# Attention with a gated residual on one core: five loads held until the third query group, and the last stores issued by ACT

## Chip, cores, metric

One Trainium2 chip, one core. The metric is the device time of one launch in microseconds. Lower is better. A profile belongs to one execution.

## The reference, cut to what matters

```python
xn  = layernorm(A_x)                       # 2048 x 448
q   = xn @ wq                              # 16 query heads of 256, 8 key/value heads
s   = softmax(q k^T / 16) v @ wo           # over the last 512 positions of the cache
g   = silu((gelu(xn @ w_gate) * (xn @ w_up)) @ w_down)
out = x + s * g
```

The gate g is worked out first and parked in DRAM. The attention then goes through four chunks of 512 rows with 16 heads each, and each chunk ends with `out = x + s*g`.

## The kernel before: the parts concerned

The kernel records operations in program order, and a helper works out the semaphore waits from the buffers. An operation therefore starts when its buffers are free, unless `after` gives it another operation to wait for.

```python
def op(self, eng, fn, reads=(), writes=(), dma=False, after=()):
    ...
    o.deps.extend(after)
```

One query group is a row of up to four pairs of q projections. Keys and values are loaded at the starts of groups. The first gates (g) and x tiles, which are read only at the ends of the first chunk (`burst_end` in the code, about 247 us), are recorded in the third group, on GpSimd's queue:

```python
if m == Q0 + QS and p == 0:                      # third group, after its first pair (m = 12)
    K.reuse(b_kT[6:] + b_va[5:] + [b for y in b_xr for b in y])
    for g in range(6, Hkv):
        load_k(g)                                # SyncE, transposing
    for g in range(5, Hkv):
        load_v(g)                                # SyncE
    for t in range(NG2):
        load_g2(t)                               # GpSimd, 2 x 112 KB
    for t in range(NXR):
        dma("pool", xr[:, t, :], x_view[:, t, :], (), b_xr[t])   # GpSimd, 3 x 112 KB
```

Recorded there, they are issued as soon as GpSimd's queue finds the buffers free. In the attention, each head's probabilities go through a transposing transfer from SBUF to SBUF on SyncE's queue (pT<-pn), two halves for each head, and the product with the values stands two heads later:

```python
dma_t(pT[:, x, t4 // 2, ...], pn[:, y, ...], (b_pn[y],), (b_pT[x][t4 // 2],))
...
if len(late) == LAG:        # LAG = 2
    pv(late.pop(0))         # reads va[g] and pT
```

The last halves of two output tiles are finished in three pieces, 224 columns of one tile and twice 112 columns of the other, each followed by its store:

```python
def last_end(t, c0, c1, i, b_i, f):
    ...
    add("dve", xs[:, t4, c0:c1], xs[:, t4, c0:c1], x[:, c0:c1], by + bx, by)
    dma("sp", out_view[:, t, c0:c1], xs[:, t4, c0:c1], by, ())
```

The pieces' (c0, c1) are (0, 224), (0, 112) and (112, 224), in this order.

The softmax here doesn't subtract the row's maximum and nothing guards it: scores larger than these inputs give would overflow.

Of the kernel before, what the change touches and what calls it, by code (L numbers as in the profile page):

```python
# [168 lines left out]
def bass_recurrent_scan__sliding_block_cached__geglu_ffn__prompt_kernel(  # L169
# [37 lines left out]
    N2 = D // 2  # L207
# [4 lines left out]
    with es:  # L212
        K = Plan(nc, es)
        base = [(nc.sbuf_base + 31) // 32 * 32]

        def place(name, shape, dt, at=None):
            size = {BF16: 2, F16: 2, F32: 4}[dt]
            for n in shape[1:]:
                size *= n
            size = (size + 31) // 32 * 32  # L220
            if at is None:
                at = base[0]
                base[0] += size
            assert at + size <= nc.sbuf_usable_end, (name, at + size, nc.sbuf_usable_end)
            return nc.alloc_sbuf_tensor_at(name, list(shape), dt, offset=at), at, at + size

        def sbuf_bufs(at, size, n):
            return [K.buf(at + i * size, size) for i in range(n)]
# [27 lines left out]
        NG2 = 2  # L256
        g2, a, _ = place("g2", [P, NG2, D], BF16)
        b_g2 = sbuf_bufs(a, D * 2, NG2)
        g2d = nc.dram_tensor("g2_all", [NT, P, D], BF16)
        b_g2d = [K.buf() for t in range(NT)]  # L260
# [8 lines left out]
        xr, a, _ = place("xr", [P, NXR, D], BF16)  # L269
        b_xr = [[K.buf(a + (i * D + lo) * 2, (hi - lo) * 2) for lo, hi in ((0, CUT), (CUT, D))] for i in range(NXR)]  # L270
# [95 lines left out]
        x_view = A_x.rearrange("b (t p) d -> p (b t) d", p=P)  # L366
        out_view = out.rearrange("b (t p) d -> p (b t) d", p=P)
# [5 lines left out]
            return n - g + (QS - Q0 if g == 0 else 0)  # L373


        def dma(q, o, i, reads=(), writes=()):
            K.op(q, lambda e, o=o, i=i: e.dma_start(o, i), reads, writes, dma=True)  # L377

        def dma_t(o, i, reads=(), writes=()):
            K.op("sp", lambda e, o=o, i=i: e.dma_start_transpose(o, i), reads, writes, dma=True)  # L380
# [4 lines left out]
        def add(eng, o, x, y, reads, writes, op=ALU.add):  # L385
            K.op(eng, lambda e: e.tensor_tensor(o, x, y, op), reads, writes)  # L386
# [10 lines left out]
        def load_x(q, t0, n):  # L397
            dma(q, x4[:, t0:t0 + n, :], x_view[:, t0:t0 + n, :], (), b_x4[t0:t0 + n])
# [185 lines left out]
        def sum_act(c, k, i=None):  # L584

            fs = {0: slice(0, 4), 1: slice(4, NH), None: slice(0, NH)}[i]
            o = lambda e, r: (actTh[:, c % 2, e * NH + fs.start:e * NH + fs.stop, r * HC:(r + 1) * HC],
                              b_actT[c % 2][e * NH + fs.start:e * NH + fs.stop])
            S = lambda j: (dn[c][0][j][0][:, fs, :], dn[c][0][j][1] if len(dn[c][0][j][1]) == 1 else dn[c][0][j][1][fs])
            j, (x, bx), (y, by), op = ((3, o(0, 0), o(0, 1), ALU.subtract), (2, o(1, 1), S(3), ALU.subtract),  # L590
                                       (0, S(2), o(0, 0), ALU.add), (1, o(1, 0), S(2), ALU.subtract))[k]
            add("dve", S(j)[0], x, y, bx + by, S(j)[1], op)
# [127 lines left out]
        def load_k(g):  # L720
            dma_t(kT[:, g, :, :], A_k_cache[0, g, Sk - W:Sk, :], (), (b_kT[g],))

        def load_v(g):
            dma("sp", va[:, g, :, :],
                A_v_cache[0, g, Sk - W:Sk, :].rearrange("(j p) d -> p j d", p=P), (), (b_va[g],))
# [90 lines left out]
        def q_group(n, pairs, more_act=False):  # L816

            c, h = divmod(n, Hq)
            units = [(b, lambda j, k, i=i: wq[:, k, (h + i) * Dh + j * P:(h + i) * Dh + (j + 1) * P],
                      wqr[:, h + i, :], slice(c * QC, (c + 1) * QC), b_wql[h // HG][:1], b_wql[h // HG][1:], b_xnT[c * 4:c * 4 + 4])  # L820
                     for i, b in enumerate(pairs)]
            group(units, 0, QC, True, True)
            for i, b in enumerate(pairs):
                s = qs(n + i)
                act(qT[:, s, 0, :], bank[b], ACT.Copy, (b_ps[b],), (b_qT[s][0],))
                if more_act and i:
                    act(qT[:, s, 1, :], bank[b + 1], ACT.Copy, (b_ps[b + 1],), (b_qT[s][1],))
                    continue
                K.op("dve", lambda v, s=s, b=b: v.tensor_copy(qT[:, s, 1, :], bank[b + 1]),  # L829
                     (b_ps[b + 1],), (b_qT[s][1],))  # L830
# [41 lines left out]
        xs = xnT[:, :, 0:D]  # L872
        o_view = oTh.rearrange("p (h e) (r q) -> p e r h q", e=2, r=2)

        def load_g2(t):
            dma("pool", g2[:, t % NG2, :], g2d[t], (b_g2d[t],), (b_g2[t % NG2],))

        def burst_end(t, ns=(0, 1)):

# [13 lines left out]
        def last_end(t, c0, c1, i, b_i, f):  # L893

            t4, x, g = t % 4, xr[:, t % NXR, :], g2[:, t % NG2, :]
            bx, by = b_xr[t % NXR][:1], [K.buf()]
            by[0].old.extend(b_xs[t4][0].readers + [b_xs[t4][0].writer])
            K.op("dve", lambda e: e.scalar_tensor_tensor(  # L898
                out=xs[:, t4, c0:c1], in0=i, scalar=f, in1=g[:, c0:c1], op0=ALU.mult, op1=ALU.mult), (b_i, b_g2[t % NG2]), by)
            add("dve", xs[:, t4, c0:c1], xs[:, t4, c0:c1], x[:, c0:c1], by + bx, by)  # L900
            dma("sp", out_view[:, t, c0:c1], xs[:, t4, c0:c1], by, ())

        def burst(c):

# [106 lines left out]
        for m in range(NS):  # L1011
            if m in groups:
                hi = groups[groups.index(m) + 1]
                three = hi - m == 6
                for i in range(m, hi, 2):
                    end = m > Hq and m % Hq == LAG
                    p = (i - m) // 2
                    q_group(i, ((cur, nxt[::-1], (cur[1], nxt[1])) if three else (cur, nxt) * 2)[p], end)
                    if m == 0:
                        sum_act(2, 2 + p)  # L1020
                    if m == Q0 and p == 0:
                        K.reuse(b_kT[2:6] + b_va[3:5])
                        for g in range(2, 6):
                            load_k(g)
                        for g in range(3, 5):
                            load_v(g)
                    if m == Q0 and p < 2:
                        gates3(2 * p)
                        gates3(2 * p + 1)
                    if m == Q0 + QS and p == 0:  # L1030
                        K.reuse(b_kT[6:] + b_va[5:] + [b for y in b_xr for b in y])
                        for g in range(6, Hkv):
                            load_k(g)
                        for g in range(5, Hkv):
                            load_v(g)
                        for t in range(NG2):
                            load_g2(t)
                        for t in range(NXR):
                            dma("pool", xr[:, t, :], x_view[:, t, :], (), b_xr[t])
                    if end and p:  # L1040
                        burst_end((m // Hq - 1) * 4 + p - 1)
                    if m > Hq and m % Hq == LAG + QS and p == 1:
                        burst_end((m // Hq - 1) * 4 + 3)
                if m == 0:
                    K.reuse([b for x in b_pT for b in x] + b_pn + b_p32)
            if m > Hq and m % Hq == LAG:
                K.reuse(b_pn + b_p32)
            s_mm(m)
            if m < LAG:
                if m == 0:  # L1050
                    gates2 = down7(2, (BB[0], BB[1], AB[2], AB[3], BB[2], BB[3]), g2w, b_g2w, (3, 4, 6, 5, 2, 1),
                                   lambda: [sum_act(3, k) for k in range(4)])
                else:
                    gates3 = down7(3, (BB[1], BB[0], AB[2], AB[3], BB[2], BB[3]), g2w, b_g2w, (3, 4, 2, 5, 6, 1),
                                   lambda: [gates2(q) for q in range(4)])
                    K.reuse(b_pT[2])
                if m == LAG - 1:
                    K.reuse(b_oT + [b for y in b_qT[:QS - Q0] for b in y])
                    assert not CASTS and not SUMS
            if len(late) == LAG:  # L1060
                pv(late.pop(0))
            if m > Hq and m % Hq == LAG - 1:
                if m // Hq == 1:
                    for b in [y for x in b_xs for y in x]:
                        b.old.extend(y for t in range(4) for z in b_xnT[t] for y in z.readers + [z.writer])
                burst(m // Hq - 1)
            late.append(m)
# [56 lines left out]
```

## Time and profile before

| | before |
|---|---|
| time, median of 4 runs with the changed kernel's | 543.56 us (543.03 to 544.43) |
| profiled span | 541.5 us |
| TensorE idle in the middle | one wait, 1.03 us, ending at 170.07 |
| last VectorE add to the span's end (called the tail from here on) | 538.93 to 541.55: 2.6 us |

The prediction shows the lines and how they are read.

### The profile page before, as it was taken

How to read it: one execution, taken by the hardware profiler on the slowest of the kernel's cores; microseconds unless marked ns; L12 is line 12 of the kernel's file. 1: busy time of each engine (PE TensorE's matmuls, PEld its weight loads, DVE VectorE, ACT ScalarE, POOL GpSimd, SP SyncE). 2: the span in 40 equal slices, each digit the busy share in tenths (PEclk: the TensorE clock that was granted, in tenths of full speed). 3: DMA queues.
4: the chain of work that ended last, by engine and by line, in shares of the span. 5: the costliest groups of instructions: out<-in, count | busy, mean ns of one | idle time of the engine just before them, and what ended most of it. 6: DMA issues, size and time to landing. Idle time of an engine off the chain costs nothing.

```text
span 541.5 us, 10848 instructions
## 1 busy us (share of the span) xinstructions
PE 535.7 (99%) x4138; PEld 306.3 (57%) x4138; DVE 376.3 (69%) x825; ACT 313.4 (58%) x780; POOL 39.5 (7%) x78
## 2 busy tenths in 40 slices
PE   8999999999999999999999999999999999999997
PEld 5554457449644444884444469544444984444587
DVE  6673885799767757934875786467667934776775
ACT  5433854873667858206875860388488216876820
POOL 1130400000002000003001000120100003001010
PEclk9999999999999999999999999999999999999999
DMA  9569261921487767302781670066457402873731
GB/s 298 120 186 130 45 142 41 301 64 42 113 189 159 157 145 149 77 1 69 164 156 45 148 146 1 18 142 153 96 105 150 67 1 72 167 151 82 135 71 35
DMA packets 171604, 61.38 MB, mean 113 GB/s; under 512 B 155104, under 2 KB 168416, under 8 KB 171552
## 3 DMA queue, kind: packets, MB, share of 16 engines
q1 hardware_dynamic: 167776, 51.39, 43.7%
q0 software_dynamic: 3008, 8.72, 6.9%
q8 instruction: 33, 0.54, 0.4%
q10 hardware_dynamic: 768, 0.57, 0.3%
q14 instruction: 19, 0.16, 0.1%
HBM read 19.76 MB, written 3.67 MB: 43 GB/s over the span
## 4 chain that ended last, share of the span: by engine, by line
PE 97%; DMA 1%; DVE 0%; issue 0%; ACT 0%; ACTq 0%
PE bank L392 97%; DMA pT<-pn 1%; DMA x<-in_A_x_dram 0%; DVE stats L439 0%; PE bank L490 0%; DVE xn L465 0%; DVE mv L442 0%; ACT p L844 0%; PE bank L509 0%; DVE xnT L898 0%; DVE xnT L386 0%; DVE rstd L459 0%; ACTq L155 0%
## 5 line engine op out<-in xcount | busy, mean ns | idle before, releaser
L844 ACT ACTIVATE p<-bank 128x512 f32<-128x512 f32 x256 | 150.6, 596 | 28.2 <-DVE pn L851 26.4
L392 PE MATMUL bank<-pT,va 128*128 128x512 bf16 x512 | 120.8, 379 | 1.0 <-DMA pT<-pn 1.0
L392 PE MATMUL bank<-kT,qT 128*128 128x512 bf16 x512 | 121.0, 379 | 0.0
L851 DVE TENSOR_SCALAR pn<-p,rden 128x512 bf16<-128x512 f32 x256 | 113.0, 484 | 8.2 <-DMA pT<-pn 3.9
L392 PE MATMUL bank<-xnT,wq 64*128 64x512 bf16 x768 | 94.9, 376 | 0.0
L392 PEld LDWEIGHTS bank<-pT,va 128*128 128x128 bf16 x512 | 49.9, 98 | 61.5 <-DMA pT<-pn 2.2
L392 PEld LDWEIGHTS bank<-kT,qT 128*128 128x128 bf16 x512 | 49.4, 98 | 61.7 <-issue 3.4
L392 PE MATMUL bank<-xnT,wgu 64*128 64x512 bf16 (+2 forms) x768 | 83.9, 350 | 0.1
L383 ACT ACTIVATE qT<-bank 128x512 bf16<-128x512 f32 x76 | 44.1, 596 | 51.9 <-PE bank L392 50.3
L829 DVE CAST qT<-bank 128x512 bf16<-128x512 f32 x52 | 34.9, 690 | 49.6 <-PE bank L392 49.6
L392 PEld LDWEIGHTS bank<-xnT,wq 64*128 64x128 bf16 x768 | 36.7, 94 | 46.3 <-ACT p L844 2.1
L392 PEld LDWEIGHTS bank<-xnT,wgu 64*128 64x128 bf16 x768 | 36.9, 94 | 36.8 <-issue 0.6
L848 DVE RECIPROCAL rden<-rsum 128x2 f32<-128x2 f32 x128 | 21.2, 165 | 47.4 <-ACT p L844 47.2
L844 ACT ACTIVATION_READ_ACCUMULATOR p<-bank 128x1 f32 x256 | 51.6, 202 | 0.0
L392 PE MATMUL bank<-wt,sr 128*128 128x224 f16 x512 | 50.0, 259 | 0.0
L383 ACT ACTIVATE gl<-bank 128x512 bf16<-128x512 f32 x56 | 33.1, 596 | 28.5 <-PE bank L392 26.1
L392 PEld LDWEIGHTS bank<-wt,sr 128*128 128x128 f16 x512 | 49.0, 98 | 0.4 <-ACT oTh L383 0.2
L869 DVE TENSOR_SCALAR oTh<-bank 128x512 f16<-128x512 f32 x62 | 42.4, 684 | 0.0
L383 ACT ACTIVATE oTh<-bank 128x512 f16<-128x512 f32 x66 | 38.9, 590 | 4.1 <-PE bank L392 4.1
L392 PE MATMUL bank<-wt,oTh 128*128 128x224 f16 (+1 forms) x416 | 38.4, 252 | 0.0
L392 PEld LDWEIGHTS bank<-wt,oTh 128*128 128x128 f16 x416 | 37.2, 98 | 0.9
L377 POOL DMA_DIRECT2D g<-g_all x14 | 7.8, 556 | 379.9 <-DVE xnT L386 285.0
(82 smaller groups left out, 403.7 us busy)
## 6 DMA issues: line engine op xcount, KB each, us to landing
wtb<-in_A_wo_dram POOLq DMA_DIRECT2D x4, 896.0 KB, 10.4
wq<-in_A_wq_dram SPq DMA_DIRECT2D x2, 1536.0 KB, 7.2
va<-in_A_v_cache_dram SPq DMA_DIRECT2D x8, 256.0 KB, 5.2
pT<-pn SPq DMA_TRANSPOSE x128, 2.7
xr<-in_A_x_dram POOLq DMA_DIRECT2D x15, 112.0 KB, 2.4
wd<-in_B_w_down_dram SPq DMA_DIRECT2D x1, 1568.0 KB, 7.9
g<-g_all POOLq DMA_DIRECT2D x14, 112.0 KB, 2.3
out_dram<-xr POOLq DMA_DIRECT2D x12, 112.0 KB, 2.2
```

What stands on the lines that cost most here:

```text
L377: K.op(q, lambda e, o=o, i=i: e.dma_start(o, i), reads, writes, dma=True)
L383: K.op("act", lambda e, o=o, i=i: e.activation(o, i, func, scale=scale), reads, writes)
L392: ins = e.matmul(o, lhsT=l, rhs=r, start=st, stop=sp, skip_group_check=True)
L829: K.op("dve", lambda v, s=s, b=b: v.tensor_copy(qT[:, s, 1, :], bank[b + 1]), (b_ps[b + 1],), (b_qT[s][1],))
L844: K.op("act", lambda e, b=b, r=r, z=z: e.activation(p32[:, z, :], bank[b], ACT.Exp, scale=att_scale, accum_out=rsum[:, r:r + 1]), (b_ps[b] ...
L848: K.op("dve", lambda e, r=r: e.reciprocal(rden[:, r - 1:r + 1], rsum[:, r - 1:r + 1]), b_rsum[r - 1:r + 1], b_rden[r - 1:r + 1])
L851: K.op("dve", lambda e, r=r - 1 + t, z=(n - 1 + t) % NP32, y=y, t=t: e.tensor_scalar(pn[:, y, t, :], p32[:, z, :], rden[:, r:r + 1], None, ...
L869: K.op("dve", lambda v, i=i, b=b: v.tensor_scalar(oTh[:, i, :], bank[b], WS, None, op0=ALU.mult), (b_ps[b],), (b_oT[i],))
```

## The change

The intent is to keep five GpSimd loads away from the transposes of the second group, and to let the last store leave without waiting for SyncE's queue. Cut to its core:

```diff
-            dma("sp", out_view[:, t, c0:c1], xs[:, t4, c0:c1], by, ())
+            dma("sp" if c1 < N2 else "act", out_view[:, t, c0:c1], xs[:, t4, c0:c1], by, ())
...
+                        now = [[o for o in K.ops if o.eng == "pe"][-1]]
                         for t in range(NG2):
-                            load_g2(t)
+                            load_g2(t, now)
                         for t in range(NXR):
-                            dma("pool", xr[:, t, :], x_view[:, t, :], (), b_xr[t])
+                            dma("pool", xr[:, t, :], x_view[:, t, :], (), b_xr[t], now)
```

`now` is the last TensorE operation recorded so far, that is the first pair of the third group. The rest of the diff passes `after` through. With N2 = 224, the first and the third store go to ACT, the second stays on SyncE.

More of the change, by code (lines that the diff above doesn't have):

```diff
@@ L373, in qs, with dma @@
             return n - g + (QS - Q0 if g == 0 else 0)
-        def dma(q, o, i, reads=(), writes=()):
-            K.op(q, lambda e, o=o, i=i: e.dma_start(o, i), reads, writes, dma=True)
+        def dma(q, o, i, reads=(), writes=(), after=()):
+            K.op(q, lambda e, o=o, i=i: e.dma_start(o, i), reads, writes, dma=True, after=after)
         def dma_t(o, i, reads=(), writes=()):
@@ L873, in bass_recurrent_scan__sliding_block_cached__geglu_ffn__prompt_kernel, with load_g2 @@
         o_view = oTh.rearrange("p (h e) (r q) -> p e r h q", e=2, r=2)
-        def load_g2(t):
-            dma("pool", g2[:, t % NG2, :], g2d[t], (b_g2d[t],), (b_g2[t % NG2],))
+        def load_g2(t, after=()):
+            dma("pool", g2[:, t % NG2, :], g2d[t], (b_g2d[t],), (b_g2[t % NG2],), after)
         def burst_end(t, ns=(0, 1)):
```

## The prediction

> **What bounds the kernel now.** I read the page first: the busy shares and the chain of work that ended last.
>
> ```profile
> PE 535.7 (99%) x4138; PEld 306.3 (57%) x4138; DVE 376.3 (69%) x825; ACT 313.4 (58%) x780; POOL 39.5 (7%) x78
> PEclk9999999999999999999999999999999999999999
> PE 97%; DMA 1%; DVE 0%; issue 0%; ACT 0%; ACTq 0%
> ```
>
> TensorE is busy for 535.7 of 541.5 us at full granted clock, and the chain is 97% matmul. Everything that can be won without fewer matmuls lies in the 5.8 us when TensorE is idle: the start, holes in the middle, and the end. Neither half of the change touches a matmul, so I looked for the holes. The list of TensorE's waits has one in the middle, and the chain in order of time says where it stands:
>
> ```profile
> PE bank L392 <- DMA pT<-pn: 1.0, 1, 1.0
> ```
>
> ```profile
> 164.73 5.29 DMA pT<-pn
> 170.02 0.05 issue
> 170.07 368.31 PE bank L392 x2592
> 538.37 0.02 issue
> 538.40 0.29 DVE xnT L898
> 538.68 0.02 issue
> 538.71 0.22 DVE xnT L386
> ```
>
> The columns are start, duration, what. One transposing transfer of the attention probabilities (pT<-pn) took 5.29 us; page part 6 gives 2.7 us as the median of all 128. After it, TensorE runs for 368 us without a hole, so the stall and the tail after 538.4 are the only two places where this change can act. The timeline around the stall shows what else was under way:
>
> ```profile
> 162.59 1.32 POOL L377 DMA_DIRECT2D g<-g_all  x2 [94.99 <-DVE rden L848]
> 163.90 1.59 POOL L377 DMA_DIRECT2D xr<-in_A_x_dram  x3
> ...
> 170.07 1.90 PE L392 MATMUL bank<-pT,va 128*128 128x512 bf16 x8 [1.03 <-DMA pT<-pn]
> ```
>
> GpSimd issues exactly the five loads that the change moves at 162.6 to 165.5, and the transposes issued at 163.28 and 164.73 fall among them; TensorE then waits 1.03 us. The DMA view of the slice 166.5 to 167.5 shows who had the DMA engines (queue, packets, MB, share of 16 engines):
>
> ```profile
> q0 software_dynamic: 31, 0.08, 46.1%
> q1 hardware_dynamic: 14, 0.00, 0.9%
> ```
>
> GpSimd's queue q0 is moving data while the transposes' q1 is all but at a standstill. So I take the five loads as the cause of the stall. Nothing reads them before the first burst end at about 247 us, so their delay costs nothing by itself.
>
> **What the Trainium skill says.** All three points are from "DMA: Bandwidth & Descriptors". Its section "Anatomy of one DMA — SWDGE (gpsimd) path" puts a GpSimd transfer at about 2.0 us plus bytes over 436 GB/s, so 2.3 us for 112 KB; the medians in the trace agree, 2.3 us for g and 2.4 us for xr. The three xr loads at 164 us took 4.1 to 4.3 us, so these were not alone. Its section "Queues, rings and completion order" says that each DMA engine goes round-robin between queues, a packet at a time. The slice above is less even than that, 46.1 to 0.9, so I can't count on fair sharing. Its section "Issuing engines are not separate DMA queues" says that another issuing engine saves only sequencer time to initiate. That is exactly what the second part of the change can win, so the question is how much SyncE time stands in front of the last store.
>
> **Part 1, what it removes.** The instruction order of the two programs differs on GpSimd only in what the first loads wait for: TensorE's semaphore instead of VectorE's; no instruction moves on TensorE or VectorE. Without the loads the transpose issued at 164.73 should land after 2.7 us, at 167.4. The matmul that needs it would follow the scores that run from 167.15 to 169.04. That is 1.6 us of room, so the whole stall goes: -1.03 us.
>
> **Part 1, what it adds.** The loads now wait for the last matmul of the first pair of q projections in the third query group. In the trace of before this pair ends near 192.3 (pairs take 3.02 us, the ACT copies of their results start at 191.76, 194.78 and 197.80). So the loads would be issued from 192.4 to about 195.1 on that scale. There they meet other transfers, as the timeline shows:
>
> ```profile
> 191.45 2.65 SPq L380 DMA_TRANSPOSE kT<-in_A_k_cache_dram  x2
> 194.14 1.68 SPq L377 DMA_DIRECT2D va<-in_A_v_cache_dram  x3
> 198.34 1.90 PE L392 MATMUL bank<-kT,qT 128*128 128x512 bf16 x8
> 200.08 1.89 PE L392 MATMUL bank<-pT,va 128*128 128x512 bf16 x8
> ```
>
> These are the keys of key/value heads 6 and 7 and the values of 5, 6 and 7. The matmul at 200.08 belongs to query head 10, two behind the scores of head 12; its key/value head is 5, so it reads the first of these three va loads. The tile view gives 4.2 us from its issue at 194.14 to its landing, so it lands at 198.3 and has only 1.7 us of room. The kT load needed at 198.34 lands at 195.3 (3.8 us after 191.45), 3 us of room. Other va loads are needed 7 us later. No pT is issued between 190.16 and 201.39, which must be why this place was chosen.
>
> How late will the va load be? The five loads' own DMA work: in the slice 162 to 168 q0 moved 0.51 MB in 45.2% of 6 us, 2.7 us of all 16 engines, so about 3.0 us for 0.57 MB. The DMA share from 193 to 198 in the view by stretches is 0.85 to 1.07 in every microsecond, so there are no free slots to take this up. By likeness: the pT transfer issued 2.1 us after the first load was late by 5.29 - 2.7 = 2.6 us; va is issued 1.7 us after the first load. The extremes are 3.0 us (all of q0's work goes first) and 1.5 us (even sharing). I choose 2.3 us, which is 0.6 us more than the room: +0.6 us of new TensorE stall, between 0 and 1.3.
>
> **Part 2, the tail.** The last three stores are ready at 537.64, 538.14 and 538.93, when the VectorE adds end. SyncE issues them in turn:
>
> ```profile
> 538.16 1.17 SPq L377 DMA_DIRECT2D out_dram<-xnT  x1
> ```
>
> The others took 0.33 and 0.43 us of the sequencer. The slow one is why the last store goes out at 539.38, not at 538.95; the tile view gives 1.6 us to its landing, 540.95, and the span ends at 541.5. One instruction fetch lies in this stretch (q8, one packet of 0.02 MB), and the store issued at 537.05 also took 2.9 us against 1.6 of its neighbour, so one held-up DMA engine is the likely reason, which blocked SyncE's queue. In the changed kernel the first and the third of these stores stand on ACT, whose last work is long past and whose two issues have no other DMA near. The third then leaves at 538.95 and lands at about 540.5. The middle one stays on SyncE and lands at 538.16 + 2.3 = 540.45 as before, so the gain can't exceed 0.5 us: -0.4 us.
>
> **Sum.** 543.99 - 1.03 + 0.6 - 0.4 = 543.16, so 543.1.
>
> **Rivals.** (a) No new stall. Work for va is queued while only g loads are in flight, and the DMA share can go above 1 (1.4 was seen at 166 to 167), so some overlap is possible; the kernel gains the full 1.4 us: 542.5 to 542.6. Against: the room is 1.7 us and the only measured likeness says 2.6. (b) The stall only moves. va comes 3 us late, TensorE waits 1.3 us at 200 us and the first half turns into a small loss: 543.9. For it: q1's starvation. (c) The tail gives nothing, because the held-up DMA engine delays ACT's stores just as well (its ring lies on the same engines): 0.4 us more than otherwise, 543.5. Against: the last store is issued only after the fetch has probably ended. (d) The hole at 170 remains since pT was late for another reason, such as the four g_all stores at 157 to 160. They take 2.9 to 4.9 us and are down by 163, so I give this little.
>
> **Range and chances.** Three runs of before span 543.13 to 544.43, so a median of few runs moves by perhaps 0.5 us. The mechanisms go from -1.5 to +0.3 us. Range 542.0 to 544.2. Two per cent are 10.9 us; nothing here is near that in either direction, unless a load waits in a way that I overlooked: same 0.98, faster 0.01, slower 0.01.
>
> **What will show it.** The timeline of the changed kernel should have the five GpSimd loads from about 191.3 (1.03 us earlier than on the scale of before). TensorE's waits should no longer have a pT wait near 169, and the two transposes there should land in 2.7 us. A wait for va of 0 to 1.3 us at about 199 decides between my sum and rivals (a) and (b); without it I sized the va delay wrong. On the tail, the last ACT store should be issued within 0.1 us of the last VectorE add, and the span should end some 2.2 us after that add, not 2.6. I am wrong altogether if the pT hole stays, or if a hole opens at the first burst end for late g or xr.

## The result, and the profile after

| | before | after |
|---|---|---|
| time, median | 543.56 us | 542.70 us (542.17 to 543.01, 4 runs) |
| ratio | | 0.9982, 95% interval 0.9964 to 1.0 |
| profiled span | 541.55 | 540.64 |
| tail | 2.6 us | 2.5 us |

A ratio is the mean time of one kernel's runs over that of the other's of the same rounds, so not quite the ratio of the medians. 0.9982 of 543.6 is 0.98 us less; the prediction's terms summed to 0.83 us less.

The page after, busy shares and chain:

```profile
PE 533.5 (99%) x4113; PEld 306.1 (57%) x4138; DVE 376.2 (70%) x825; ACT 313.3 (58%) x780; POOL 39.4 (7%) x78
PE 98%; issue 0%; DMA 0%; DVE 0%
```

The DMA's 1% has left the chain. TensorE's busy time fell by 2.2 us, but not because work went: 25 of its matmul records are missing from this trace (x4113, while the weight loads are still x4138). TensorE's waits after show the same loss:

```profile
PE bank L509 <- DVE epst L423: 1.2, 1, 1.2
PE bank L392 <- ACT qT L383: 1.0, 6, 0.2
PE bank L392 <- issue: 0.5, 3, 0.2
PE bank L490 <- DVE xn L465: 0.5, 1, 0.5
```

The pT wait is not there. The waits of 0.2 us for ACT and "issue" stand where a first matmul has no record, and are no new waits: the weight loads at these places are as far apart as before. The timeline of TensorE where the hole was:

```profile
168.89 1.89 PE L392 MATMUL bank<-pT,va 128*128 128x512 bf16 x8
170.62 1.89 PE L392 MATMUL bank<-kT,qT 128*128 128x512 bf16 x7
```

The product that started at 170.07 before starts at 168.89, 1.18 us earlier. (The hole reads as 1.03 us in the list of waits because a matmul's modelled end, 1.89 us for eight, lies beyond the start of the next, which follows 1.72 us after; the profile's pauses are a little too short.) The transposes issued there now land in time (view of tile pT, 160 to 170 us):

```profile
DMA to landing us min/median/max: 2.7/2.8/2.9
```

The five loads are where the prediction put them, and GpSimd waited for TensorE. This is the GpSimd timeline after, then SyncE's and TensorE's at the same place:

```profile
191.48 1.10 POOL L377 DMA_DIRECT2D g<-g_all  x2 [123.85 <-PE bank L392]
192.57 1.59 POOL L377 DMA_DIRECT2D xr<-in_A_x_dram  x3
...
193.05 1.70 SPq L377 DMA_DIRECT2D va<-in_A_v_cache_dram  x3
...
198.89 1.89 PE L392 MATMUL bank<-pT,va 128*128 128x512 bf16 x8
```

There is no wait at 198.89, the product that needs the first va load. The tile view gives 5.3 us from its issue at 193.05 to its landing, so it came at 198.4, 1.1 us later after its issue than before (4.2 us), and there were 0.5 us left.

The tail after (timeline), in which ACT issues the first and third store:

```profile
536.84 1.99 ACTq L377 DMA_DIRECT2D out_dram<-xnT  x2
537.09 0.22 DVE L386 TENSOR_TENSOR xnT<-xnT,xr 128x112 bf16<-128x112 bf16 x1
537.33 0.33 SPq L377 DMA_DIRECT2D out_dram<-xnT  x1
537.57 0.28 DVE L898 SCALAR_TENSOR_TENSOR xnT<-bank,g 128x112 bf16<-128x112 f32 x1 [0.26 <-PE bank L392]
537.88 0.22 DVE L386 TENSOR_TENSOR xnT<-xnT,xr 128x112 bf16<-128x112 bf16 x1
```

The last store was issued at once after the last add (538.13), but the issue took 0.70 us and the landing 1.9 us, not 1.6. The tail shrank from 2.6 to 2.5 us only.

So the span's 0.91 us are made up thus: 1.18 us at the hole; minus 0.36 us lost again on the way, since the last VectorE product starts at 537.57 against 538.40, only 0.83 us earlier; plus 0.1 us of tail. More than half of the 0.36 us lies at one place: the pT product that follows the one at 271.83 before (270.64 after, 1.19 us earlier) started at 275.28 before and at 274.31 after, 0.97 us earlier. There a pT came late in the kernel after (landed at 274.26), with an instruction fetch in flight at 271.0. In the kernel before, transposes took up to 4.5 us to land there too, with a fetch at 271.6, and were just in time. Whether the fetch delays them is not shown.

### The profile page after: what moved, and what is told of

Its sections match the earlier page's. It is cut to its first block, busy times and chain, and to the rows that moved or that the text cites. A ratio compares the mean times of both kernels' runs of the same rounds, so it can differ in the third digit from the quotient of the medians.

```text
span 540.6 us, 10823 instructions
## 1 busy us (share of the span) xinstructions
PE 533.5 (99%) x4113; PEld 306.1 (57%) x4138; DVE 376.2 (70%) x825; ACT 313.3 (58%) x780; POOL 39.4 (7%) x78
## 4 chain that ended last, share of the span: by engine, by line
PE 98%; issue 0%; DMA 0%; DVE 0%
PE bank L392 98%; DMA x<-in_A_x_dram 0%; DVE stats L439 0%; PE bank L490 0%; DVE xn L465 0%; DVE mv L442 0%; PE bank L509 0%; DVE xnT L898 0%; DVE xnT L386 0%; DVE rstd L459 0%
## 5 line engine op out<-in xcount | busy, mean ns | idle before, releaser
L392 PE MATMUL bank<-kT,qT 128*128 128x512 bf16 x487 | 117.8, 379 | 2.3 <-ACT qT L383 1.0
```

The lines of the kernel that those rows point to most:

```text
L392: ins = e.matmul(o, lhsT=l, rhs=r, start=st, stop=sp, skip_group_check=True)
```

## The experiments

Twelve runs, five of which repeat a kernel. Kernels are compared only within the same rounds. "Hole" is the pT wait of TensorE near 169 us, by the list of waits.

| run | loads at 162 us | last stores | hole, us | tail, us | ratio to before (95%) |
|---|---|---|---|---|---|
| before (first profile) | g, x | SyncE | 1.0 | 2.6 | |
| after | none | ACT, SyncE | none | 2.5 | 0.9982 (0.9964 to 1.0) |
| e1_loads_only | none | SyncE | none | 3.4 | 0.9983 (0.997 to 0.9995) |
| e2_store_only | g, x | ACT, SyncE | 0.3 | 2.4 | 0.9984 (0.9969 to 0.9999) |
| e3_g_early | g | ACT, SyncE | none | 2.5 | 0.9977 (0.9962 to 0.9992) |
| e4_x_early | x | ACT, SyncE | 0.3 | 2.3 | 0.9985 (0.9968 to 1.0001) |
| e5_changed_again | none | ACT, SyncE | none | 2.05 | 0.9982 (0.997 to 0.9994) |
| e6_fetch_shift | none | ACT, SyncE | none | 2.0 | 0.9992 (0.998 to 1.0004) |
| e7_fetch_shift_sp | none | SyncE | none | 2.4 | 1.0004 (0.9991 to 1.0017) |
| e8_va_last | none | ACT, SyncE | none; va wait 1.2 | 2.5 | 1.0002 (0.9989 to 1.0015) |
| e9_before_again | g, x | SyncE | 0.2 | 2.75 | 0.9998 (0.9983 to 1.0014) |
| e10_loads_only_again | none | SyncE | none | 2.8 | 0.9974 (0.9956 to 0.9991) |
| e11_store_only_again | g, x | ACT, SyncE | 0.9 | 2.6 | 0.9999 (0.998 to 1.0017) |
| e12_changed_third | none | ACT, SyncE | none | 2.6 | 0.9974 (0.9958 to 0.999) |

### Each part alone

e1_loads_only is the changed kernel with this line put back:

```diff
-            dma("sp" if c1 < N2 else "act", out_view[:, t, c0:c1], ...)
+            dma("sp", out_view[:, t, c0:c1], ...)
```

> Part 1 alone: the five loads held, all last stores on SyncE as before. Theory (the two parts act apart, the hole at 170 us was the five loads'): the pT wait of 1.03 us is gone, TensorE ends 0.8 to 1.2 us earlier than before, and the tail from the last VectorE add to the span's end stays at 2.5 to 2.7 us; time 0.7 to 1.0 us below before. Rival (the stores' new queue is what removed time, or the pT was late for the stores of the gates): no gain, the hole stays.

Measured: the hole is gone, the last VectorE add ends at 538.13 against 538.93, and the time is 0.92 us below before (0.0017 of 543.7). The tail of this profile is 3.4 us, outside what I expected. SyncE's three last stores in the timeline show why:

```profile
536.87 2.90 SPq L377 DMA_DIRECT2D out_dram<-xnT  x3
```

In the trace's own records the first of the three issues took 1.95 us, while one 16 KB instruction fetch (536.78, 1.65 us long) was in flight. The profile fell on the slowest of this kernel's five runs (543.40; the other four lie between 542.47 and 542.92), so it is not typical.

e2_store_only is the kernel before with only the store's line of the change.

> Part 2 alone: loads early as before, the two last stores on ACT. Theory: the hole of 1.0 us at 170 us stays, and the tail from the last VectorE add to the span's end is 2.45 to 2.6 us instead of 2.6, so the time is at most 0.2 us below before. Rival (my prediction's tail): the tail is 2.2 us, 0.4 us gained; the changed kernel's 2.5 us would then have been bad luck with its instruction fetch.

Measured: TensorE's waits again hold a pT wait, but a smaller one than in the first profile of the same loads:

```profile
PE bank L392 <- DMA pT<-pn: 0.3, 1, 0.3
```

The tail is 2.4 us. The time was 0.87 us below before, far more than I expected of 0.2 us, with an interval that nearly reaches 1. Its six runs range from 542.09 to 543.88. So either the hole is often small, or this is chance.

### Which loads make the hole

e3_g_early: `load_g2(t)` in place of `load_g2(t, now)`, x held. e4_x_early: the x loads first and without `now`, g held:

```diff
+                        for t in range(NXR):
+                            dma("pool", xr[:, t, :], x_view[:, t, :], (), b_xr[t])
                         for t in range(NG2):
                             load_g2(t, now)
-                        for t in range(NXR):
-                            dma("pool", xr[:, t, :], x_view[:, t, :], (), b_xr[t], now)
```

> As the changed kernel, but the two g loads stay where they were (162.6 us), only the three x loads are held. If the x loads alone starved the transposes (they had the DMA engines when q1 stood still): no pT wait at 170, transposes there land within 3.5 us, time as the changed kernel. If any load does it: a wait of 0.3 to 0.6 us.

> As the changed kernel, but the three x loads stay early and the two g loads are held. If the x loads did it: a pT wait of 0.5 to 1.0 us near 170, time 0.5 to 1.0 us above the changed kernel. If the harm is in proportion to the bytes (3 of 5): the transposes are late by 1.5 us, which is within the 1.6 us of room, and there is no wait.

Measured: with the g loads early and the x loads held, no pT wait, and the transpose issued next to 164.9 lands in 2.8 us. With the x loads early, a wait of 0.3 us, and the same transpose takes 4.6 us to land. View of tile pT, 164.6 to 165.2 us, e3 and then e4:

```profile
DMA to landing us min/median/max: 2.7/2.8/2.8
DMA to landing us min/median/max: 4.6/4.6/4.6
```

The lateness is 4.6 - 2.7 = 1.9 us, and the room 1.6 us, which leaves the 0.3 us. So the x loads do it; the wait is smaller than I expected for them (0.5 to 1.0 us), and the times of the two (0.9977 and 0.9985) are too close to tell apart. In all five profiles with the x loads early, the late transpose lands 0.8 to 1.2 us after the last of the x loads (trace records). What the two runs don't separate is the kind of load from its moment: in e3 the g loads are down by 164.9, as this transpose is issued, while the x loads are issued beside the transposes (163.4 to 164.8 in e4).

### Is the room at 199 us real?

e5_changed_again is the changed kernel unaltered. e8_va_last changes one order:

```diff
-                        for g in range(5, Hkv):
+                        for g in (6, 7, 5):
                             load_v(g)
```

> The changed kernel once more, for a second profile. Theory: no pT wait near 169, TensorE ends 0.4 to 0.9 us before that of the kernel before, tail 2.3 to 2.6 us; time 0.8 to 1.2 us below before. A wait near 199 for the values (my prediction's new stall) would show that the first profile was lucky: the room left there was 0.6 us.

> The changed kernel with the three va loads of the third query group issued in the order 6, 7, 5, so that the one needed first comes last. Theory (the held loads push the va loads back by 1.1 us, which the room of 1.7 us hides): the load for head 5 lands near 200.1 us, the matmul that needs it stood at 199.0, so TensorE waits 0.9 to 1.2 us for va there. Rival (the held loads don't compete with va): it lands by 199.0 and TensorE waits at most 0.1 us.

Measured: e5 has no va or pT wait, and its first va load took 5.2 us (trace records), like the 5.3 us of the first profile. Its tail was 2.05 us, shorter than I expected. In e8, TensorE's waits hold exactly the wait that the prediction had feared:

```profile
PE bank L392 <- DMA va<-in_A_v_cache_dram: 1.2, 1, 1.2
```

The last of its three va loads landed at 200.07 us (trace records). The ratio went from 0.9982 (e5) to 1.0002, 1.1 us of 543, and the runs of the two don't overlap (542.03 to 542.49 against 542.74 to 543.49), so the whole gain of the change was lost for the order of three loads. In the kernel before, the last of the three landed at 199.9 us (4.6 us after 195.3) for a product at 200.08: the same order would just have fitted there. The held loads do compete with va, and the order va 5, 6, 7 is what hides it.

How much they compete is seen from the DMA view of five microseconds in each kernel, from 1.1 us before the first va load is issued: 193 to 198 before and 192 to 197 after (queue, packets, MB, share of 16 engines). Before, then after:

```profile
DMA packets 3229, 1.10 MB, mean 219 GB/s; under 512 B 2081, under 2 KB 3229, under 8 KB 3229
q1 hardware_dynamic: 3229, 1.10, 100.0%
```

```profile
DMA packets 2416, 1.12 MB, mean 224 GB/s; under 512 B 2012, under 2 KB 2277, under 8 KB 2416
q1 hardware_dynamic: 2215, 0.62, 61.2%
q0 software_dynamic: 201, 0.50, 48.5%
```

The engines move hardly more with the loads than without, 1.12 against 1.10 MB: what q0 moves, 0.50 MB, q1 moves less, 0.48 MB. So the loads took their bytes from q1 one for one. The other profiles agree: from 1 us before the first va load to 4 us after it, 1.11 to 1.20 MB in the four with all loads early and 0.96 to 1.18 MB in the eight with all held. (A window of six microseconds misleads here: before, the transfers run out in the sixth, which makes its rate look low.) The delay is spread: against the kernel before, the second kT load landed 1.55 us later after its issue and the three va loads 1.1, 1.2 and 1.3 us later.

The 1.1 us compare two profiles. Over all of them, the first va load of the three takes 3.2 to 4.2 us in the four with all loads early and 5.2 to 5.6 us in the eight with all loads held (trace records; in e8 it is that of head 6), 1.7 us more on average. The product follows the issue by 5.6 to 5.95 us where it does not wait, so it had 0.3 to 0.8 us left in the seven that issue the needed load first.

### The instruction fetch and the tail

e6_fetch_shift and e7_fetch_shift_sp are the changed kernel and e1's kernel with

```diff
-        warm(9, 2, QC)
+        warm(34, 2, P)
```

which takes 25 more, narrower warm-up matmuls, so that every fetch of TensorE's instructions comes earlier in the kernel.

> The changed kernel with 34 warm-up matmuls of 128 columns in place of 9 of 512, 25 matmuls more, so that every 16 KB fetch of TensorE's instructions falls some 25 matmuls earlier: the last one near 534.5 us, before the last stores. Theory (the fetch holds one DMA engine and with it the last stores): every one of the last four stores lands in 1.5 to 1.7 us, the tail is 2.1 to 2.25 us, 0.3 to 0.4 us less than the changed kernel; the time less by as much, unless a fetch now meets a pT elsewhere. Rival (stores queue up behind each other): landings of 2 to 3 us and a tail of 2.4 us or more remain.

> The same shift with the stores all on SyncE. Theory: without the fetch SyncE's issues take 0.33 to 0.45 us each and no store is blocked, so the tail is 2.1 to 2.3 us here too, and ACT's queue is worth nothing. Rival (SyncE's queue is full by itself): one issue of about 1.2 us remains and the tail is over 2.5 us.

Measured: the last fetch moved to 534.9 us in e6 and 534.5 us in e7 (trace records, 1.4 us long both times), ahead of the last three stores. The slow stores moved with it: in e7 those issued at 533.5 to 534.5 us now take 3.1 to 3.5 us to land, and one issue 1.84 us. In e7 SyncE's three last issues take 0.43 us each and land in 1.6 us each:

```profile
L377 SPq DMA_DIRECT2D out_dram<-xnT x3: 430/430/430, 537.3 to 538.2; - x3
DMA to landing us min/median/max: 1.6/1.6/1.6
```

None is blocked. The tail is 2.4 us, just above the 2.3 us that I expected, because SyncE still works off stores that the earlier fetch held up and issues the last one 0.2 us after its add. In e6, with ACT, the tail is 2.0 us. Its last four stores land in 1.84, 1.95, 1.66 and 1.50 us, so two miss the 1.5 to 1.7 us that I expected of every one. So the fetch is what made the landings and issues long, and my rivals for these two runs (stores that queue up behind each other, a queue full by itself) fall. As a version it is no good: the ratios are 0.9992 and 1.0004, against 0.9982 for e5. TensorE's timeline of e6 has the price:

```profile
12.99 0.39 PE L392 MATMUL bank<-xnT,wgu 64*128 64x256 bf16 x4 [0.41 <-issue]
```

TensorE stands 0.4 us (0.27 us in e7) with nothing to wait for that the profile shows. By its weight loads it falls 0.60 us (0.46 us in e7) behind the changed kernel at this place and stays behind. Whether it waits for instructions there is not shown: the two fetches nearby, at 10.3 and 14.1 us, are not in flight in the pause, and the changed kernel has them too (10.5 and 14.5 us). The pause takes back what the tail gave, and e7's runs scatter up to 543.79 for reasons that its one profile doesn't show.

### Do the parts add up?

e9 is the kernel before, e10 that of e1, e11 that of e2, e12 the changed kernel.

> The kernel before itself, for a second profile and to see what the comparison says of two equal kernels. The hole near 170 us was 1.0 us in its first profile, but 0.3 us in the two later kernels that issue the x loads early. If it is 1.0 us as a rule here: again 0.9 to 1.1 us. If it varies from run to run: anything from 0.2 to 1.1. Tail 2.6 to 3.4 us (SyncE's store held up by the instruction fetch). The ratio is within 0.1% of 1.

> Part 1 alone once more, on one chip with the others. If the two parts add up: no pT wait near 169, tail 2.6 to 3.4 us, time 0.4 to 0.8 us below before and 0.2 to 0.6 us above both parts together.

> Part 2 alone once more. If the two parts add up: a pT wait of 0.3 to 1.0 us near 169, tail 2.0 to 2.6 us, time 0.2 to 0.6 us below before. In its first timing it stood 0.9 us below, as much as both parts together; if that comes again, the hole costs nothing in most executions.

> Both parts, on one chip with each part alone: no pT wait near 169, tail 2.0 to 2.55 us, time 0.8 to 1.2 us below before and below either part alone by 0.2 us or more.

Measured: 543.80, 542.43, 543.60 and 542.36 us (medians). Part 1 alone has the same ratio as both parts, 0.9974. Part 2 alone has 0.9999, so its 0.87 us did not come again. My expectation that e10 would stand 0.2 to 0.6 us above e12 is not met: the two differ by 0.07 us. Nor are the sizes: by the ratios e10 and e12 are 1.41 us below before (0.4 to 0.8 and 0.8 to 1.2 expected), and e11 0.05 us (0.2 to 0.6 expected).

The second profile of the kernel before has two pT waits instead of one (waits, then TensorE's timeline):

```profile
PE bank L392 <- DMA pT<-pn: 1.2, 2, 1.0
```

```profile
169.40 1.90 PE L392 MATMUL bank<-pT,va 128*128 128x512 bf16 x8 [0.21 <-DMA pT<-pn]
363.33 1.90 PE L392 MATMUL bank<-pT,va 128*128 128x512 bf16 x8 [1.00 <-DMA pT<-pn]
```

The hole at 169 is 0.2 us this time and another of 1.0 us has opened at 363, in the middle of the third chunk. GpSimd had issued one x load at 358.88 us there, between two transposes (358.46 and 360.10), the first of which took 4.8 us to land. It looks like the same meeting at another place; but in the first profile of before the same load is issued at 358.81 us, and the transposes beside it land in 3.5 and 3.8 us with no wait. No run here removes that load, so this stays open.

## Why the prediction was right, and where it was not

The time (543.1 predicted, 542.7 measured, range 542.0 to 544.2) held. The single steps fared less evenly, and that the time came so close is in part luck.

**The hole is from the five loads, and goes.** Right. In eight profiles with the x loads held there is no pT wait at 169 (after, e1, e3, e5, e6, e7, e10, e12; e8 makes nine); in all five with the x loads early there is one. e3 and e4 narrow it to the three x loads. Rival (d), pT late for the gates' stores, is dead: these stores stand in all of them. What I took too simply is the size. The -1.03 us came from one profile, and the five profiles give 1.03, 0.31, 0.30, 0.21 and 0.88 us, by how late the transpose lands (4.5 to 5.3 us against 4.3 that it may take, 2.7 + 1.6). One trace gives the mechanism, not its mean.

**+0.6 us of new wait for va.** This step failed: "I choose 2.3 us, which is 0.6 us more than the room". Against the trace that I started from, the va load came 1.1 us late, inside the 1.7 us of room, so there was no new wait. That is rival (a) in its outcome, but not in its reason: the engines moved no more than without the loads, and the five loads took their bytes from q1 one for one. What was mis-sized is how much of this falls on the first va load. I had set the extremes at 1.5 us (even sharing) and 3.0 us (all of q0 first); the other transfers on q1 were delayed as well, and the first va load by 1.1 us against the one trace, 1.7 us on the average of the profiles. The 4.2 us of my trace were the longest of four (3.2 to 4.2). And the likeness that I used for 2.3 us was a transpose from SBUF to SBUF that met reads from HBM, while the va load is itself a plain read; whether that is why it failed is not shown. The danger was real all the same, as e8 shows: with the load for head 5 issued last the wait is 1.2 us and the gain is gone.

**-0.4 us of tail.** Right in its mechanism, wrong in its size. The last store did leave at once, and a fetch was what held up SyncE's queue (e7). I had written that ACT's two issues "have no other DMA near". They had: the fetch (537.0 us, 1.44 us long in the trace records) is in flight while both are under way, and as both queues' stores are late together I infer that it holds a DMA engine that both use. ACT's first store lands in 2.9 us and its second issue takes 0.70 us. That was rival (c). The tail fell by 0.1 us in the first pair of profiles. Over all profiles without the shifted fetch it is 2.6, 2.75, 2.8 and 3.4 us with SyncE and 2.05 to 2.6 us with ACT (eight profiles), so something is gained on average, some 0.4 us. The times don't bear it out: part 2 alone gives 0.9984 and 0.9999, and e10 against e12 shows no difference. What part 2 is worth in time stays open; by the tails it is between nothing and half a microsecond.

**The sum.** -0.83 us forecast, -0.98, -0.98 and -1.41 us measured for both parts (three ratios), -0.92 and -1.41 us for part 1 alone. Two wrong terms, +0.6 that didn't come and -0.4 that was mostly not there, partly cancelled: that is luck. (I started from 543.99 us, the median of three runs; the comparison has 543.56 for before, and that is where most of the difference between 543.1 and 542.7 comes from.) In the first comparison the interval still reaches 1.0; in the repeats, e5 and e12, it does not.

Where the gain lies can be read from TensorE's weight loads, which all traces hold completely, by laying the traces over each other (trace records). Measured so, against the nine profiles with the x loads held, the stall at 169 us is 1.20, 0.38, 0.49, 1.05 and 0.48 us in the five profiles with the x loads early (before, e9, e2, e11, e4), where the list of waits has 0.2 us less each. At the end of its work TensorE is 1.06 us earlier on average in after, e1, e5, e10 and e12 than in before, e9, e2 and e11. Some 0.8 us of this is the stall at 169 us, and most of the rest is one stall in one profile, e9's at 363 us, which no run explains. So the measured gain is about what TensorE gains, but the parts vary: two executions of one kernel can differ by as much as the whole change.

## What to carry to other kernels

When a chain is all TensorE, look for single holes and ask which early transfer, needed by nobody yet, was in flight; hold it for a place where no urgent transfer runs, and issue the urgent ones in the order in which they are needed. When the DMA engines are full, suspect that added transfers take their bytes from the others, as here (compare the bytes moved while both still have work), and ask how late the first one needed lands and what room it has. Take the size of a hole from several profiles before it becomes a term of a sum.

## What the Trainium skill lacked or had wrong

- "Runtime: NRT & Kernel Launch", section "Instruction fetch mechanics", says that instructions come in 16 KiB blocks of 256, with a cost that is mostly hidden. The runs agree on the size (33 fetches, 0.54 MB, in the page's queue table). They show a cost that the page doesn't mention: while a block of 0.9 to 1.7 us was under way, stores that land in 1.6 us took 2.0 to 3.8 us, and a SyncE issue of 0.33 us took 1.2 to 1.95 us.
- "DMA: Bandwidth & Descriptors", section "Issuing engines are not separate DMA queues": another engine saves only the time to initiate. The runs agree, and add that this time is not always small: a second issuing engine avoids a blocked issue of up to 1.95 us, but its own issue still took up to 0.70 us during a fetch.
- The same page, section "Queues, rings and completion order": round robin between queues, a packet at a time. The runs don't contradict it, but packets say little of shares of time. Of the packets begun from 166.5 to 167.5 us, with the x loads under way, q0 had 31 and q1 14; their shares of the engines' time were 46.1% and 0.9%, and with packets that had begun earlier q0 held 89% (trace records). So the prediction's "less even than that" compares two different things.
- How a transpose fares beside a GpSimd read from DRAM is on no page that I read: 4.5 to 5.3 us to land instead of 2.7 for the one that TensorE waited for.
